# Going through eight weight columns in two runs of four instead of one run of eight

## The chip, the cores and the metric

The kernel runs on one core of a Trainium2 chip. The core has a matmul engine (TensorE, PE in the profile; its loads of stationary weights are PEld), three engines for elementwise work (VectorE or DVE, ScalarE or ACT, GpSimd or POOL) and SyncE (SP), which issues all DMAs here. Each engine works through its own instructions in order; semaphores order them between engines. The metric is the time of one execution on the device in microseconds, the median of several runs.

## The reference, cut to what matters

```python
def sm_attn(qq, kk, vv):                       # softmax(scale * qq kk^T) vv
    s = scale * np.matmul(qq, kk.transpose(0, 1, 3, 2))
    a = np.exp(s - np.max(s, axis=-1, keepdims=True))
    return np.matmul(a / (np.sum(a, axis=-1, keepdims=True) + 1e-09), vv)

p_packed = sm_attn(p, k, v)                    # 32 packed tokens per head
x = sm_attn(q, p_packed, p_packed)             # 8 batches, 8 heads, 576 tokens, 64 wide
x = x.transpose(0, 2, 1, 3).reshape(4608, 512)
h = x @ w_in                                   # 512 -> 2048
x = (np.maximum(h, 0) + alpha * np.minimum(h, 0)) @ w_out       # 2048 -> 512
g = x @ w_gate                                 # 512 -> 1536
return (g / (1 + np.exp(-g)) * (x @ w_val)) @ w_out2            # 1536 -> 512
```

The weights come as 64-bit floats. The kernel makes 32-bit floats of them on the chip and then splits each into a high and a low part, so that three fast matmuls (high by high, low by high, high by low) give a product of nearly full precision.

## The kernel before, in words

**Tiling.** The 4608 tokens are taken as 16 half batches `j` of 288 tokens, two for each of the 8 batches. The 2048 columns of the first layer are 16 blocks `f` of 128. A unit is one pair (`j`, `f`): `h_unit` (line 983) makes h for 128 columns and 288 tokens with 6 matmuls, ACT makes `m` (line 1003), DVE makes `g` (line 1006), ACT and POOL split g (lines 1014 and 1016), and three iterations later `o_unit` (line 1019) multiplies g by 128 rows of `w_out` with 12 matmuls into four PSUM banks `acc0` to `acc3`. The list `order` (line 872) says which units follow each other; there are 256.

**Projection.** The attention's second product is folded into the first layer: `pp_win(b, j)` (line 773) multiplies the packed tokens of batch b by four columns f of `w_in` and leaves a high and a low part (`ppw`). In the scripts `w02` means batch 0, columns 8 to 11, `w03` columns 12 to 15. There are four buffers of `ppw`.

**Runs.** The first two batches (four half batches) are computed while `w_in` and `w_out` are still being converted, so they don't go through all 16 columns at once. They go through columns 0 to 7 for each of the four half batches (units 0 to 31) and then through columns 8 to 15 (units 32 to 63). At the end of a run (`stop`) the four banks are evicted: at the end of a first run ACT and DVE copy them (lines 1051 and 1049) and SP stores them as partial sums `x1p` (line 1052); for the second run `load_part` (line 978) loads the partial sums back (line 981), DVE adds the banks to them (line 1047) and SP stores the result `x1d`. The tiles for this have the tag `x` with two buffers, which one half batch uses both. The first `o_unit` of a new run is put off by one iteration, so that the eviction has time. The later batches go through all 16 columns in one run.

**Conversion.** `convert()` (line 269) takes the next of 32 pieces (16 of `w_in`, 16 of `w_out`, in the order of `ORDER`), each 512 KB: a DMA (line 217), one or two ACT operations, five DVE operations (lines 224, 228, 237, 246, 254; pieces in `BY_POOL` have the last one on ACT and POOL), a POOL addition (line 265), and for `w_out` two ACT operations and a POOL operation more (lines 283 to 285). The work space is three raw buffers and five value buffers in `raw_tiles` and in one tile of tag `v`. `HOLD` puts the first ACT operation of some pieces behind the `m` of a given unit.

**Order of the work.** `EARLY` is a script by (iteration, 0 before or 1 after the `h_unit`): a `1` converts one piece, `w..` is a projection, the others are steps of the attention of batches 0 and 1. The attention of batch 2 is spread over units 36 to 62 by `STEPS`. A scheduler that simulates the engines sets the order of instructions within each engine from this program order, so a step can run some iterations away from its place. From iteration `CHAIN0` = 36 on every step is issued only behind the previous unit's `m` and `g` and the rounding of the one before (line 1288). From half-iteration `GROUP0` = 84 on (iteration 42) `more_weights2` (line 962) converts the second layer's weights in steps, up to two in each half-iteration, in the scratch of the first conversion, and stores them to DRAM (`wgvd`, `wo2d`); a tile of that scratch's tag is used again for the second layer's input at half-iteration 489.

Of the kernel before, what the change touches and what calls it, by code (L numbers as in the profile page):

```python
# [8 lines left out]
F32 = mybir.dt.float32  # L9
# [8 lines left out]
P = 128  # L18
# [27 lines left out]
    (13, 0): "d.a2",  # L46
    (15, 0): "c.a2",
    (17, 1): "w11",
    (18, 1): "1 1",
    (20, 1): "1 1",  # L50
    (21, 1): "1",
    (23, 1): "1",
    (24, 1): "1",
    (25, 1): "1 1",
    (26, 1): "1 1",
    (27, 1): "1 w02",
    (28, 1): "w03",
    (33, 1): "1",
    (36, 1): "w12 w13",
    (37, 1): "1 1",  # L60
}

ORDER = """
    i2 o2 i0 i3 i1 o0 o3 o1 i5 i4 i7 i6 o5 o4 o7 o6
    i13 i10 i11 o13 i15 i8 i14 i9 i12 o10 o14 o8 o9 o12 o11 o15
"""

BEHIND = {"c.k": 3, "c.q": 4, "c.v": 5, "d.k": 5, "d.q": 6, "d.v": 9}

BY_POOL = {0, 2, 4, 7, 11, 18, 23, 29}  # L70
HOLD = {15: 5, 16: 7, 17: 15, 19: 16}


STEPS = """
# [12 lines left out]

GROUP0 = 84  # L90


FIRST_X = dict(load=-36, A11=-27, S=-26, S2=-25, A12=-12, D4=-11, S3=-11, S1=-10, A22=-8, S4=-7)
# [11 lines left out]
def f32(ap):  # L105
    return ap.bitcast(F32)
# [3 lines left out]
def tile_kernel(  # L110
# [24 lines left out]
    B, H, S, D = q.shape  # L135
    NP = p.shape[2]
    NT, DM = out.shape
    KC = DM // P
    NF1 = alpha.shape[0] // P
# [6 lines left out]
    HS = S // 2  # L146
    NBLK = NT // (2 * T)
    NQ = H // HQ
    NHALF = 2 * B
# [3 lines left out]
    dram = ctx.enter_context(tc.tile_pool(name="dram", bufs=1, space=DRAM))  # L153
# [16 lines left out]
    def utile(tag, shape, name, dt=F32):  # L170
        return upool.tile(shape, dt, tag=tag, name=name, bufs=UBUFS[tag])
# [32 lines left out]
    def like(ap, other):  # L204

        return ap if len(other.shape) == 2 else ap.rearrange("p (c f) -> p c f", c=KC)
# [4 lines left out]
    def use(*cut):  # L211
        raws[:] = sum((r for r, _ in cut), [])
        vals[:] = sum((v for _, v in cut), [])

    def widen(src, raw, val, out=None, n_piece=-1):

        issued.append(nc.sync.dma_start(out=like(raw, src), in_=src))
        words = raw.rearrange("p (n t) -> p n t", t=2)
        low, high = words[:, :, 0], words[:, :, 1]
        held = n_piece in HOLD  # L220
        with tc.issue_after(begun[HOLD[n_piece]].ins) if held else ExitStack():
            nc.scalar.activation(out=f32(val), in_=f32(high), func=AF.Abs)
        yield "v"
        nc.vector.tensor_scalar(
            out=f32(val), in0=f32(val), scalar1=E_TOP, scalar2=E_LOW, op0=ALU.min, op1=ALU.max
        )
        yield "v"
        nc.vector.tensor_scalar(
            out=val,
            in0=val,  # L230
            scalar1=3,
            scalar2=0x3FFFFFF8,
            op0=ALU.logical_shift_left,
            op1=ALU.bitwise_and,
        )
        yield "v"
        nc.vector.scalar_tensor_tensor(
            out=val,
            in0=high,
            scalar=0xC0000000,  # L240
            in1=val,
            op0=ALU.bitwise_and,
            op1=ALU.bitwise_or,
        )
        yield "v"
        nc.vector.tensor_scalar(
            out=high, in0=val, scalar1=0xFF800000, scalar2=None, op0=ALU.bitwise_and
        )
        yield "v"
        if n_piece in BY_POOL:  # L250
            nc.scalar.activation(out=f32(low), in_=low, func=AF.Copy, scale=2.0**-52)
            nc.gpsimd.tensor_tensor(out=f32(low), in0=f32(low), in1=f32(high), op=ALU.mult)
        else:
            nc.vector.scalar_tensor_tensor(
                out=f32(low),
                in0=low,
                scalar=2.0**-52,
                in1=f32(high),
                op0=ALU.mult,
                op1=ALU.mult,  # L260
            )
        yield "p"
        full = f32(val) if out is None else like(f32(val), out)
        other = f32(low) if out is None else like(f32(low), out)
        nc.gpsimd.tensor_tensor(  # L265
            out=full if out is None else out, in0=full, in1=other, op=ALU.add
        )

    def convert(n=1):

        for src, parts, f in queue[:n]:
            raw, val = raws.pop(0), vals.pop(0)
            raws.append(raw)
            vals.append(val)
            n_piece = len(issued)
            dst = parts()
            light = len(dst) == 1
            for _ in widen(src, raw, val, dst[0] if light else None, n_piece):
                pass
            if not light:  # L280
                hi, lo = dst
                full = like(f32(val), hi)
                nc.scalar.activation(out=full, in_=full, func=AF.Copy, scale=sg[:, f : f + 1])
                nc.scalar.activation(out=hi, in_=full, func=AF.Copy)
                nc.gpsimd.tensor_tensor(out=lo, in0=full, in1=f32(hi), op=ALU.subtract)
        del queue[:n]
# [7 lines left out]
    def cut_up(t, raws):  # L294

        n = t.shape[1]
        return (
            [t[:, 1024 * i : 1024 * (i + 1)] for i in range(raws)],
            [t[:, c : c + 512] for c in range(1024 * raws, n, 512)],
        )  # L300
# [248 lines left out]
    def behind():  # L549

        return tc.issue_after(before[-1].ins) if before else ExitStack()

    def done(last):
        if chained:
            before[:] = [last]
# [250 lines left out]
    for f in range(NF1):  # L806
# [4 lines left out]
    space = cut_up(raw_tiles[0], 2), cut_up(raw_tiles[1], 1)  # L811
# [4 lines left out]
        b=quad(1, ["h"], evac=nc.vector),  # L816
# [11 lines left out]
    def run(script):  # L828
        for word in script.split():
            if word == "1":  # L830
                convert()
            elif word[0] == "w":
                pp_win(int(word[1]), int(word[2]))
            else:
                n, step = word.split(".")
                if step == "pd":
                    groups[n][step](pd[:, dense[n][0], :], dense[n][1])
                else:
                    groups[n][step]()
# [26 lines left out]
    def at(it, late, fn):  # L866

        plan.setdefault((it, late), []).append(fn)

    order = []
    for bs in [(0, 1)] + [(b,) for b in range(2, B)]:
        for fs in (range(NF1 // 2), range(NF1 // 2, NF1)) if len(bs) > 1 else (range(NF1),):
            for j in range(2 * bs[0], 2 * bs[-1] + 2):
                order += [(j, f, f == fs[0], f == fs[-1]) for f in fs]

    NB1 = 2 * NF1
    busy = set()
# [96 lines left out]
    x1p = {}  # L976

    def load_part(j):
        part[j] = [utile("x", [P, 2, HS], f"x1p{j}_{pr}") for pr in range(2)]
        for pr in range(2):  # L980
            nc.sync.dma_start(out=part[j][pr], in_=x1p[j][:, 2 * pr : 2 * pr + 2, :])
# [37 lines left out]
    def o_unit(it):  # L1019
        j, f, start, stop = order[it]  # L1020
        ghi, glo = gs.pop(it)
        hi, lo = wout[f // WP]
        for dc in range(KC):
            if start:
                acc[dc] = ps.tile([P, 512], F32, tag=f"acc{dc}", name=f"acc{dc}_{it}")[:, :HS]
        with behind():
            for dc in range(KC):
                c = slice(dc * P, (dc + 1) * P)
                nc.tensor.matmul(acc[dc], lo[:, f % WP, c], ghi, start=start, stop=False)  # L1029
                last = nc.tensor.matmul(acc[dc], hi[:, f % WP, c], ghi, start=False, stop=False)  # L1030
        done(last)
        with behind():
            for dc in range(KC):
                c = slice(dc * P, (dc + 1) * P)
                last = nc.tensor.matmul(acc[dc], hi[:, f % WP, c], glo, start=False, stop=stop)  # L1035
        done(last)
        if not stop:
            return
        if f != NF1 - 1:
            x1p[j] = dram.tile([P, KC, HS], F32, name=f"x1p{j}")  # L1040
        dst = x1d[j] if f == NF1 - 1 else x1p[j]
        for pr in range(2):
            xs = part[j][pr] if j in part else utile("x", [P, 2, HS], f"x1s{it}_{pr}")
            for i in range(2):
                a = acc[2 * pr + i]
                if j in part:
                    nc.vector.tensor_tensor(out=xs[:, i, :], in0=a, in1=xs[:, i, :], op=ALU.add)
                elif i:
                    nc.vector.tensor_copy(out=xs[:, i, :], in_=a)
                else:  # L1050
                    nc.scalar.activation(out=xs[:, i, :], in_=a, func=AF.Copy)
            nc.sync.dma_start(out=dst[:, 2 * pr : 2 * pr + 2, :], in_=xs)

    for j in range(4):
        at(NB1 + 8 * j + 6, 0, lambda j=j: load_part(j))


    raw2, xs2, gvw, wo2, ps2, acc2, outs = {}, {}, {}, {}, {}, {}, {}
# [229 lines left out]
    def steps(it, late):  # L1288


        with ExitStack() as held:
# [6 lines left out]
            slot = 2 * it + late  # L1298
            if slot >= GROUP0:
                more_weights2(slot not in busy)  # L1300
# [59 lines left out]
```

## Time and profile before

| | us |
|---|---|
| median of 3 runs | 1701.05 |
| lowest and highest | 1701.03 and 1706.88 |
| the profiled execution, whole | 1702.91 |
| its span in the trace | 1701.1 |
| PE busy | 1609.9 (95%) |
| DVE busy | 868.2 (51%) |
| ACT busy | 683.0 (40%) |
| POOL busy | 708.8 (42%) |

The span runs from the first to the last instruction. Busy time of an engine doesn't say what bounds a stage; for this the idle time of the engine that does the most, and what ended it, is read by stretch. In this document stretches are cut at 139.85, 192.63, 246.41 and 281 us, where the activation of line 1003 of units 18, 34, 51 and 63 starts. The granted clock (PEclk) is the share of full speed that the matmul engine got.

### The profile page before, as it was taken

How to read it: one execution, taken by the hardware profiler on the slowest of the kernel's cores; microseconds unless marked ns; L12 is line 12 of the kernel's file. 1: busy time of each engine (PE TensorE's matmuls, PEld its weight loads, DVE VectorE, ACT ScalarE, POOL GpSimd, SP SyncE). 2: the span in 40 equal slices, each digit the busy share in tenths (PEclk: the TensorE clock that was granted, in tenths of full speed). 3: DMA queues.
4: the chain of work that ended last, by engine and by line, in shares of the span. 5: the costliest groups of instructions: out<-in, count | busy, mean ns of one | idle time of the engine just before them, and what ended most of it. 6: DMA issues, size and time to landing. Idle time of an engine off the chain costs nothing.

```text
span 1701.1 us, 28474 instructions
## 1 busy us (share of the span) xinstructions
PE 1609.9 (95%) x10708; PEld 1456.6 (86%) x10708; DVE 868.2 (51%) x1549; ACT 683.0 (40%) x1511; POOL 708.8 (42%) x752
## 2 busy tenths in 40 slices
PE   5688899999999989999899999999999999999997
PEld 3467798988888888889899999999999999999997
DVE  6999757565756656565533443443443343244222
ACT  5774645555544555454522232232232232123122
POOL 3556744565554654547622322322322222232222
PEclk7799999999999999999999999999999999999999
DMA  9433464635445362644573463465455456445442
GB/s 238 121 102 115 120 159 115 165 95 155 130 108 143 117 156 53 150 138 139 182 274 141 177 237 139 166 202 185 164 211 182 158 191 202 159 174 185 156 173 81
DMA packets 227369, 266.11 MB, mean 156 GB/s; under 512 B 130464, under 2 KB 189856, under 8 KB 227232
## 3 DMA queue, kind: packets, MB, share of 16 engines
q1 hardware_dynamic: 227232, 264.30, 49.2%
q8 instruction: 84, 1.38, 0.3%
q14 instruction: 53, 0.43, 0.1%
HBM read 214.70 MB, written 49.55 MB: 155 GB/s over the span
## 4 chain that ended last, share of the span: by engine, by line
issue 39%; PE 25%; POOL 17%; DMA 7%; DVE 6%; ACT 4%; SPq 1%; POOLq 0%; ACTq 0%; DVEq 0%
POOL pl L1247 8%; PE acc L1029 5%; PE acc L1030 5%; PE acc L1035 5%; POOL s L1227 4%; DMA wgvd<-cva 4%; PE h L305 3%; PE h L307 2%; PE h L306 2%; POOL lo L1016 1%; DMA cva<-in_moe_w_gate_dram 1%; POOL cva L934 1%; DVE g L1006 1%; PE ppw L564 1%; POOL cva L265 1%
## 5 line engine op out<-in xcount | busy, mean ns | idle before, releaser
L1016 POOL TENSOR_TENSOR lo<-g,hi 128x288 fp32r<-128x288 f32 x256 | 227.5, 890 | 240.6 <-ACT hi L1014 187.8
L1227 POOL TENSOR_TENSOR s<-s,u 128x384 f32<-128x384 f32 x72 | 73.0, 1014 | 489.9 <-ACT s L1221 489.9
L1006 DVE SCALAR_TENSOR_TENSOR g<-h,sg,m 128x288 f32<-128x288 f32 x256 | 130.3, 509 | 162.2 <-ACT m L1003 132.0
L1184 DVE TENSOR_TENSOR u<-yb,p 128x384 f32<-128x384 f32 x144 | 80.1, 556 | 255.6 <-PE yb L307 255.6
L1247 POOL TENSOR_TENSOR pl<-s,ph 128x384 fp32r<-128x384 f32 x144 | 145.5, 1032 | 106.4 <-ACT ph L1245 106.4
L305 PE MATMUL h<-a2h,ppw 128*128 128x288 f32 x512 | 163.2, 319 | 27.0 <-DVE g L1006 21.4
L1184 DVE TENSOR_TENSOR u<-vb,u 128x384 f32<-128x384 f32 x144 | 80.4, 558 | 197.3 <-PE vb L307 196.9
L1014 ACT ACTIVATE hi<-g 128x288 fp32r<-128x288 f32 x256 | 113.1, 442 | 155.5 <-DVE g L1006 149.1
L307 PE MATMUL o<-wp,ph 128*128 128x512 f32 x432 | 171.5, 397 | 0.0
L306 PE MATMUL o<-wp,ph 128*128 128x512 f32 x432 | 170.9, 396 | 0.0
L305 PE MATMUL o<-wp,pl 128*128 128x512 f32 x432 | 168.8, 391 | 0.9 <-POOL pl L1247 0.9
L1221 ACT ACTIVATE s<-p 128x384 f32<-128x384 f32 x72 | 37.9, 526 | 302.0 <-DVE p L1184 302.0
L307 PE MATMUL h<-a2l,ppw 128*128 128x288 f32 x512 | 153.0, 299 | 0.0
L306 PE MATMUL h<-a2h,ppw 128*128 128x288 f32 x512 | 152.5, 298 | 0.0
L305 PEld LDWEIGHTS h<-a2h,ppw 128*128 128x128 f32 x512 | 97.9, 191 | 62.4 <-DVE g L1006 33.0
L305 PE MATMUL yb<-ring,gv 128*128 128x384 f32 x432 | 146.0, 338 | 0.2
L307 PE MATMUL yb<-ring,gv 128*128 128x384 f32 x432 | 144.4, 334 | 0.0
L306 PE MATMUL yb<-ring,gv 128*128 128x384 f32 x432 | 144.4, 334 | 0.0
L1003 ACT ACTIVATE m<-h,sal 128x288 f32<-128x288 f32 x256 | 125.6, 492 | 41.5 <-PE h L307 40.6
L1245 ACT ACTIVATE ph<-s 128x384 fp32r<-128x384 f32 x144 | 69.8, 519 | 121.3 <-DVE s L1225 121.3
L307 PEld LDWEIGHTS h<-a2l,ppw 128*128 128x128 f32 x512 | 98.0, 191 | 0.8 <-issue 0.8
L306 PEld LDWEIGHTS h<-a2h,ppw 128*128 128x128 f32 x512 | 98.4, 192 | 0.0
(232 smaller groups left out, 4187.1 us busy)
## 6 DMA issues: line engine op xcount, KB each, us to landing
gv<-wgvd SPq DMA_DIRECT2D x144, 896.0 KB, 6.2
wgvd<-cva SPq DMA_DIRECT2D x84, 256.0 KB, 2.6
cva<-in_moe_w_out_dram SPq DMA_DIRECT2D x28, 512.0 KB, 3.8
v<-in_v_dram SPq DMA_DIRECT2D x16, 576.0 KB, 5.4
out_dram<-os SPq DMA_DIRECT2D x12, 768.0 KB, 3.8
cva<-in_moe_w_in_dram SPq DMA_DIRECT2D x16, 512.0 KB, 3.9
kr<-in_k_dram SPq DMA_DIRECT2D x96, 72.0 KB, 2.8
qr<-in_q_dram SPq DMA_DIRECT2D x96, 72.0 KB, 2.5
```

Of the source, the lines that this page charges most:

```text
L305: nc.tensor.matmul(o, wlo, xhi, start=start, stop=False, **kw)
L306: nc.tensor.matmul(o, whi, xhi, start=False, stop=False, **kw)
L307: return nc.tensor.matmul(o, whi, xlo, start=False, stop=stop, **kw)
L1003: begun[it] = nc.scalar.activation(out=m, in_=hp, func=AF.Copy, scale=sal[:, f : f + 1])
L1006: made[it] = nc.vector.scalar_tensor_tensor(out=g32, in0=hp, scalar=sg[:, f : f + 1], in1=m, op0=ALU.mult, op1=ALU.max)
L1014: rounded[n] = nc.scalar.activation(out=hi, in_=x, func=AF.Copy)
L1016: nc.gpsimd.tensor_tensor(out=lo, in0=x, in1=f32(hi), op=ALU.subtract)
L1029: nc.tensor.matmul(acc[dc], lo[:, f % WP, c], ghi, start=start, stop=False)
L1030: last = nc.tensor.matmul(acc[dc], hi[:, f % WP, c], ghi, start=False, stop=False)
L1184: return nc.vector.tensor_tensor(out=out, in0=bank, in1=x, op=ALU.add)
L1227: latest.append(nc.gpsimd.tensor_tensor(out=s2, in0=s2, in1=u3, op=ALU.mult))
L1247: nc.gpsimd.tensor_tensor(out=lo, in0=x, in1=f32(hi), op=ALU.subtract)
```

## The change

The list of units of the first two batches is given by a table `RUNS`: columns 0 to 7 of the four half batches, then 8 to 11 of the four, then 12 to 15 of the four. Each half batch now ends three runs instead of two; the end after column 11 adds to the partial sums and stores them again under a new DRAM name. A `load_part` is placed at the iteration of the last unit of each run after the first (units 35, 39, 43, 47 and 51, 55, 59, 63) instead of at iterations 38, 46, 54 and 62. The conversions from iteration 18 on are spread differently, the projections `w02`, `w03`, `w12` and `w13` move, a word `D` takes the tile of tag `v` out of the work space at iteration 37, columns 8 to 11 are converted before 12 to 15, one `HOLD` is two units later, and `GROUP0` is 90 instead of 84 (iteration 45).

```diff
     (17, 1): "w11",
-    (18, 1): "1 1",
-    (20, 1): "1 1",
+    (18, 1): "1",
+    (20, 1): "1",
     (21, 1): "1",
     (23, 1): "1",
     (24, 1): "1",
-    (25, 1): "1 1",
-    (26, 1): "1 1",
-    (27, 1): "1 w02",
-    (28, 1): "w03",
-    (33, 1): "1",
-    (36, 1): "w12 w13",
-    (37, 1): "1 1",
+    (25, 1): "1",
+    (26, 1): "w02",
+    (27, 1): "1",
+    (29, 1): "1",
+    (31, 1): "1",
+    (33, 1): "1 w12",
+    (34, 1): "1",
+    (35, 1): "1",
+    (36, 1): "1",
+    (37, 0): "D",
+    (39, 1): "1",
+    (41, 1): "1 w03",
+    (43, 1): "1",
+    (50, 1): "w13",
 }
 ORDER = """
     i2 o2 i0 i3 i1 o0 o3 o1 i5 i4 i7 i6 o5 o4 o7 o6
-    i13 i10 i11 o13 i15 i8 i14 i9 i12 o10 o14 o8 o9 o12 o11 o15
+    i8 i9 i10 i11 o8 o9 o10 o11 i12 i13 i14 i15 o12 o13 o14 o15
 """
-HOLD = {15: 5, 16: 7, 17: 15, 19: 16}
+HOLD = {15: 5, 16: 7, 17: 15, 19: 18}
+
+RUNS = ((0, 1, 2, 3), 0, 8), ((0, 1, 2, 3), 8, 12), ((0, 1, 2, 3), 12, 16)
-GROUP0 = 84
+GROUP0 = 90
+            elif word == "D":
+                use(*space)
-    order = []
-    for bs in [(0, 1)] + [(b,) for b in range(2, B)]:
-        for fs in (range(NF1 // 2), range(NF1 // 2, NF1)) if len(bs) > 1 else (range(NF1),):
-            for j in range(2 * bs[0], 2 * bs[-1] + 2):
-                order += [(j, f, f == fs[0], f == fs[-1]) for f in fs]
+    order, again = [], []
+    for js, f0, f1 in RUNS + tuple(((j,), 0, NF1) for j in range(4, NHALF)):
+        for j in js:
+            if f0:
+                again.append((len(order) + f1 - f0 - 1, j))
+            order += [(j, f, f == f0, f == f1 - 1) for f in range(f0, f1)]
         if f != NF1 - 1:
-            x1p[j] = dram.tile([P, KC, HS], F32, name=f"x1p{j}")
+            x1p[j] = dram.tile([P, KC, HS], F32, name=f"x1p{j}_{f}")
-    for j in range(4):
-        at(NB1 + 8 * j + 6, 0, lambda j=j: load_part(j))
+    for it, j in again:
+        at(it, 0, lambda j=j: load_part(j))
```

## Rows read from the trace of the kernel before

**Rows 1.** The page: the span, and each engine's busy time.
```profile
span 1701.1 us, 28474 instructions
...
PE 1609.9 (95%) x10708; PEld 1456.6 (86%) x10708; DVE 868.2 (51%) x1549; ACT 683.0 (40%) x1511; POOL 708.8 (42%) x752
```

**Rows 2.** Stretches: us, busy us (xinstructions) by engine, granted clock, DMA share, GB/s.
```profile
139.85:192.63 52.78, 45.63 (x305) 39.52 (x304) 47.31 (x70) 29.40 (x62) 37.22 (x32) 0.97 0.39 122
192.63:246.41 53.78, 49.15 (x461) 43.45 (x467) 31.09 (x65) 29.46 (x70) 27.37 (x31) 1.00 0.59 141
246.41:281.00 34.59, 34.34 (x298) 29.93 (x284) 25.39 (x46) 18.64 (x41) 19.93 (x23) 1.00 0.51 146
sum 141.15, PE 129.12 PEld 112.91 DVE 103.78 ACT 77.50 POOL 84.52; mean PE 43.04 PEld 37.64 DVE 34.59 ACT 25.83 POOL 28.17
```

**Rows 3.** Waits of PE, 139.85 to 281: waiter, releaser, us, times, longest.
```profile
PE h L305 <- DVE g L1006: 5.1, 6, 2.2
PE ppw L795 <- DVE ppw L800: 3.5, 2, 3.0
PE acc L1029 <- DVE x1s L1049: 3.0, 1, 3.0
```

**Rows 4.** Timeline of PE: start, us, instruction [idle before, releaser].
```profile
161.83 0.40 PE L305 MATMUL h<-a2h,ppw 128*128 128x288 f32 x1 [2.16 <-DVE g L1006]
...
167.42 0.37 PE L1029 MATMUL acc<-hi,wo0l 128*128 128x288 f32 x1 [3.04 <-DVE x1s L1049]
...
200.04 1.08 PE L795 MATMUL ppw<-wi,ppT 128*64 128x512 f32 x4 [3.05 <-DVE ppw L800]
```

**Rows 5.** Stretches of 1 us after 168, and 200 to 204.
```profile
168.00:169.00 1.00, 1.00 (x5) 0.38 (x5) 1.00 (x4) 0.23 (x1) 0.00 (x0) 0.54 0.84 317
...
171.00:172.00 1.00, 1.00 (x6) 0.25 (x3) 0.93 (x3) 1.00 (x3) 1.00 (x1) 0.76 0.00 0
...
200.00:204.00 4.00, 3.50 (x18) 1.81 (x19) 4.00 (x9) 1.24 (x3) 0.00 (x0) 1.00 0.89 222
```

**Rows 6.** DVE by line, 139.85 to 192.63: busy us, mean ns, idle before.
```profile
L254 DVE SCALAR_TENSOR_TENSOR cva<-cva 128x512 f32<-128x512 uint32 x8 | 7.5, 938 | 0.0
...
L237 DVE SCALAR_TENSOR_TENSOR cva<-cva,cva 128x512 uint32<-128x512 uint32 x1 | 1.2, 1164 | 0.0
```

**Rows 7.** DVE by line, 192.63 to 246.41.
```profile
L254 DVE SCALAR_TENSOR_TENSOR cva<-cva 128x512 f32<-128x512 uint32 x4 | 3.1, 801 | 0.0
...
L237 DVE SCALAR_TENSOR_TENSOR cva<-cva 128x512 uint32<-128x512 uint32 x2 | 1.4, 682 | 0.0
```

**Rows 8.** Additions of partial sums: the group (ns), and three run ends in the timeline.
```profile
L1047 DVE TENSOR_TENSOR x1p<-acc,x1p x16: 420/448/457, 223.3 to 295.6; 128x288 f32<-128x288 f32 x16
...
223.33 1.54 DVE L1047 TENSOR_TENSOR x1p<-acc,x1p 128x288 f32<-128x288 f32 x4
...
245.16 1.55 DVE L1047 TENSOR_TENSOR x1p<-acc,x1p 128x288 f32<-128x288 f32 x4
...
269.92 1.51 DVE L1047 TENSOR_TENSOR x1p<-acc,x1p 128x288 f32<-128x288 f32 x4
```

**Rows 9.** Timeline of SP: issues of stores and loads of partial sums.
```profile
224.17 1.07 SPq L1052 DMA_DIRECT2D x1d<-x1p  x2
226.31 1.09 SPq L981 DMA_DIRECT2D x1p<-x1p  x2
...
249.79 1.69 SPq L981 DMA_DIRECT2D x1p<-x1p  x2
...
275.35 0.33 SPq L981 DMA_DIRECT2D x1p<-x1p  x1
```

**Rows 10.** The tile x1p, 212 to 300: from issue to landing.
```profile
DMA to landing us min/median/max: 2.1/2.7/3.9
```

**Rows 11.** Waits of SP's queue, 212.62 to 281.
```profile
SPq L1052 <- DVE x1p L1047: 17.9, 4, 8.6
```

**Rows 12.** Last store of the second layer's weights (SP), first product after (PE).
```profile
845.61 1.66 SPq L947 DMA_DIRECT2D wo2d<-cva  x2
...
859.46 0.34 PE L305 MATMUL xb<-ring,gv 128*128 128x384 f32 x1
```

## The prediction

> **What bounds the kernel now.** The page comes first: the span is 1701.1 us and the matmul engine (PE) is busy 95% of it [rows 1]. So a change can only win where PE stands idle, or runs at half clock. The diff touches the first 64 units (a unit is one `h_unit` and, three iterations later, one `o_unit`), so the next view is the busy time by stretch, cut at the starts of units 18, 34, 51 and 63 [rows 2]. In the first stretch PE is busy 45.63 of 52.78 us while VectorE (DVE) is busy 47.31: idle 7.15 us. In the second it is idle 53.78 - 49.15 = 4.63, in the third 0.25. Together 12.0 us of 141.15; this is nearly all that the change can win. The waits of PE say what ends the idle time [rows 3]: 5.1 us for `g` from DVE (line 1006), 3.5 us for the residual of a projected weight from DVE (line 800), 3.0 us for the eviction of a run's sums by DVE (line 1049). All three are DVE. The timeline shows the three largest gaps: 2.16 us before a unit at 161.83, 3.04 us at a run's end at 167.42, 3.05 us between the two projections of unit 36 at 200.04 [rows 4]. [...]
>
> What fills DVE: ten rows of the first stretch belong to weight conversion (lines 224 to 254; 7.5 us down to 1.2 us, 39.0 us in all, about 9 pieces, 4.3 us a piece) ([rows 6], first and last of the ten). In the second stretch six such rows sum to 11.0 us for 4 pieces, 2.75 us a piece ([rows 7], first and last of the six).
>
> **The change, part by part.**
>
> *Conversions moved (first stretch).* Before, the script starts 11 pieces from iteration 18 to 26, then 2 by 33, then 2 at 37. After, it is 6 by iteration 25 and 9 more from 27 to 41; the tenth, at 43, finds the queue empty. Since pieces run up to a few iterations behind their slot, I take 3 pieces out of the first stretch. [...] Idle 7.15 plus clock 1.7 is 8.9 us. It can't fall below nothing, and it can stay as it is if `g` still queues behind a conversion in DVE's order. I keep 2 us (a 0.8 us wait at some units, and part of one eviction's wait), because the third stretch, with DVE at 25.39 of 34.59 us (73%), idles 0.25 us [rows 2]. Term: -7.0, bounds -8.9 and 0.
>
> *Projections split.* `w12 w13` ran back to back at iteration 36 with two PSUM buffers, so the second waited for the evictions of the first: 3.05 us at 200.04, and 0.46 us more within the 3.5 us of line 800 [rows 3, 4]. Now `w02`, `w12`, `w03` and `w13` stand at 26, 33, 41 and 50, each alone. Their matmuls stay the same in number. Term: -3.0, bounds -3.5 and 0 (a lone one can still wait for DVE).
>
> *Conversions moved (second stretch).* The same 3 pieces come to iterations 34 to 51: +8.3 us by 2.75, +12.9 us by 4.3. They lie beside PE work, but DVE was at 31.09 of 53.78 us; with these and with 8 of the new additions (8 x 0.448 = 3.6 us [rows 8]) it comes to 43 to 47.6 us, against 49.15 us of PE work. That is 87 to 97%, as full as the first stretch was before (47.31 of 52.78, 90%, with 7.15 us idle). What speaks for less: from iteration 36 on each step is issued only behind the previous unit's `m`, `g` and rounding (`CHAIN0`), so `g` goes ahead of conversions. Bounds 0 and +8 us; I take +3.5, nearer to the third stretch's 0.25 than to 7.15.
>
> The first row of conversion says why the price of a piece differs: line 254 takes 938 ns in the first stretch and 801 ns in the second [rows 6, 7], with GpSimd (POOL) busy 37.22 of 52.78 us and 27.37 of 53.78 us [rows 2]. [...]
>
> *Four more run ends.* Each of the four half batches now ends a run after column 11 too: 4 x 4 additions x 0.448 us = 7.1 us of DVE [rows 8], 8 stores and 8 loads of 288 KB. PE gets no matmul more; it waits only if an eviction is late, since the first `o_unit` of a new run is put off by one iteration, which leaves two `h_unit`s to cover the four additions of 1.5 us. The risk is the turnaround: the `x` tiles have two buffers, both used by one half batch, so the next partial sums can be loaded only after the last ones are stored. In the trace the stores follow the first addition within 1 us and the loads are issued at 226.31, 249.79 and 275.35 [rows 9]; with a landing of 2.7 us (at most 3.9) [rows 10] the last load has landed 6.5 to 9.9 us after the first addition (223.33, 245.16, 269.92 [rows 8]). Run ends were 8 units apart, 21.8 and 24.8 us; they will be 4 apart, 10.9 to 12.4 us. So 1.0 to 5.9 us are to spare. Bounds 0 and +17 (below, second rival); I take +1.0 for the odd late one.
>
> *SP's queue.* SP issues in order; stores waited 17.9 us in 4 waits for their additions, up to 8.6 us [rows 11], and twice as many will stand there. Behind them are raw weights, K, Q and V of batch 2 and the stores of the second layer's weights. None of these shows among PE's waits [rows 3], so the cover is there; if it goes, it shows as DVE waiting for K or Q. Taken at 0 (within the bounds of the last term).
>
> *Second layer's weights three iterations later (`GROUP0`).* The scripts' last step moves by 5 half-iterations. Its last stores are issued at 845.61, the first product of the next stage starts at 859.46 [rows 12]: 13.8 us apart, while 2.5 iterations at 10.9 to 12.4 us for four are 7 to 8 us. Taken at 0, bounds -2 and +5 (all later conflicts shift in phase too).
>
> *`HOLD`, `ORDER`, the `D` word, new DRAM names:* the order only follows the runs, and `D` gives the shared scratch back before V of batch 2 is loaded. Cost 0; the cover is that columns 12 to 15 are needed only at iteration 48.
>
> Sum: -7.0 - 3.0 + 3.5 + 1.0 = -5.5 us. The profiled execution took 1702.91 us for a span of 1701.1 us (1.8 us lie around it), the median is 1701.05. So the span should be 1695.6, and the median of runs 1701.05 - 5.5 = 1695.6 us.
>
> **The rivals.**
>
> *All of the idle time goes.* The second stretch takes the added DVE work as the third took its own, with about 0 idle, and the run ends cost nothing: -7.0 - 3.0 - 1.0 (half of the 2 us kept) = -11 us, 1690 us. For it: the chained order. Against: DVE near 90% has come with idle PE elsewhere.
>
> *The stall only moves.* Total DVE work rises by 7.1 us and no piece is removed; the second stretch then idles as the first did, +8, and run ends cost 2: net 0, 1701 us. For it: 87 to 97%. Against: the chain order and the split projections, which don't depend on DVE's share.
>
> *Turnaround too long (the other side).* Place: the 7 loads of partial sums that follow another run's additions, 4 units before. If SP holds the store or load so that the turn is 13.5 us instead of 6.5 to 9.9, each end comes 2.5 us late after the spare time is used, the additions block DVE's queue and PE waits for the banks: 7 x 2.5 = 17.5, 1713 us. It decides from 0.8 us per end (5.5 / 7). For it: one hold of 8.6 us at a store. Against: holds end when the additions are done, and loads went out 2 to 5 us after them. Rows show what a late end adds beyond its idle time: after 3.04 us idle the clock fell, after 3.05 us at 200.04 it stayed at 1.00 [rows 4, 5]. [...]
>
> **How the numbers follow.** Forecast 0.45 (1691 to 1700), all idle time gone 0.25 (1690), stall only moves 0.17 (1701), turnaround 0.13 (1713). A measurement tells 0.5%, 8.5 us, from no change: faster is below 1692.5, slower above 1709.6. Faster: 0.25 and 0.07 of the forecast's low end, 0.32. Slower: 0.13. Same: 0.55. The range for 8 in 10 takes the idle time gone with the clock's 1.7 and a favourable phase (-15, 1686) and half of the turnaround's price (1707).
>
> **What would show it.** In the changed trace: PE idle from unit 18 to 34 about 2 us; no gap of 3 us between projections; idle from 34 to 51 about 5 us with DVE at 43 us or more; 32 rather than 16 additions of line 1047's kind, none waiting on a load of `x1p`. The prediction is wrong if the wait for a load ends PE's idle time at several run ends, if the first stretch still idles 6 us, or if idle time grows after unit 66.

## The result and the profile after

The changed kernel takes 1712.05 us (median of 9 runs, 1707.58 to 1719.71). The kernel before, run beside it, takes 1704.74 us (9 runs). The ratio is 1.0055, 95% interval 1.0037 to 1.0072: about 9 us slower. The forecast was 5.5 us faster, and 1712 lies above the range's upper end of 1707. The sign was wrong.

The page of the changed kernel, span and busy time by engine (its profiled execution took 1714.91 us):

```profile
span 1712.9 us, 28519 instructions
...
PE 1622.1 (95%) x10708; PEld 1465.1 (86%) x10708; DVE 873.1 (51%) x1565; ACT 683.4 (40%) x1511; POOL 704.5 (41%) x752
```

PE has the same 10708 matmuls as in [rows 1] and is busy 12.2 us longer, so it must run slower somewhere. The stretches, cut at units 18, 34, 51 and 63 of this kernel, and below them three windows of 2 us; the columns are those of [rows 2]:

```profile
138.66:192.45 53.79, 48.12 (x302) 41.10 (x301) 45.72 (x67) 26.67 (x57) 36.39 (x33) 0.94 0.38 120
192.45:256.47 64.02, 55.72 (x466) 48.57 (x472) 38.58 (x75) 30.23 (x69) 25.16 (x26) 0.89 0.58 151
256.47:290.93 34.46, 34.46 (x301) 30.27 (x294) 27.92 (x53) 19.01 (x42) 20.16 (x24) 1.00 0.62 184
...
218.00:220.00 2.00, 2.00 (x9) 2.00 (x9) 1.01 (x3) 1.06 (x3) 1.01 (x1) 0.50 0.00 0
...
248.00:250.00 2.00, 0.00 (x0) 0.00 (x0) 1.09 (x3) 1.64 (x4) 0.00 (x0) 0.92 0.15 42
...
252.00:254.00 2.00, 2.00 (x10) 2.00 (x9) 0.11 (x1) 0.28 (x1) 0.00 (x0) 0.50 0.00 0
```

The second stretch takes 64.02 us instead of 53.78; the first is 1.0 us longer and the third 0.1 us shorter. The best single measure of a stretch is what PE loses in it: its length less busy time times granted clock, so that idle time and half clock count alike. Before, this was 52.78 - 45.63 x 0.97 = 8.5, then 4.6 and 0.3 us, 13.4 in all. After, it is 53.79 - 48.12 x 0.94 = 8.6, then 64.02 - 55.72 x 0.89 = 14.4, then 0: 23.0 in all. These 9.6 us are about the measured slowdown, and all of them lie between units 34 and 51. The spans of the two profiled executions differ by 11.8 us: the changed kernel's is 1.2 us shorter before unit 18, 11.1 longer from unit 18 to 63, 2.8 shorter from there to unit 252, and 4.7 longer from unit 252 to the end. The last figure comes back under `GROUP0` below.

What PE waited for from unit 18 to 63 (columns as in [rows 3]):

```profile
PE h L314 <- DVE g L1018: 5.6, 5, 1.9
PE ppt L635 <- DVE ppw L809: 4.8, 1, 4.8
PE s L573 <- DVE ppw L809: 2.1, 1, 2.1
PE s L573 <- DVE kT L623: 1.4, 1, 1.4
```

The wait of one projection for another is gone, and so is the one for a run's eviction (3.5 and 3.0 us in [rows 3]). In their place the attention of batch 2 (`s`, `ppt`) waits for the eviction of a projection (`ppw`), 2.1 and 4.8 us. The timeline of the engines around both places shows why:

```profile
211.07 1.67 DVE L246 SCALAR_TENSOR_TENSOR cva<-cva,cva 128x512 uint32<-128x512 uint32 x1
212.78 0.91 DVE L255 TENSOR_SCALAR cva<-cva 128x512 uint32<-128x512 uint32 x1
213.72 0.69 DVE L263 SCALAR_TENSOR_TENSOR cva<-cva 128x512 f32<-128x512 uint32 x1
...
214.76 0.68 DVE L809 TENSOR_TENSOR ppw<-ppw,ppw 128x512 fp32r<-128x512 f32 x1
...
215.49 2.27 PE L573 MATMUL s<-kT,pT 64*32 64x288 f32 x16 [2.05 <-DVE ppw L809]
...
242.05 0.38 SPq L226 DMA_DIRECT2D cva<-in_moe_w_val_dram  x1
...
244.82 1.94 PE L804 MATMUL ppw<-wi,ppT 128*64 128x512 f32 x8
...
248.20 0.66 ACT L231 ACTIVATE cva<-cva 128x512 f32<-128x512 f32 x1 [5.01 <-DMA cva<-in_moe_w_val_dram]
...
249.15 0.59 ACT L808 ACTIVATE ppw<-ppw 128x512 fp32r<-128x512 f32 x1
...
251.57 0.48 PE L635 MATMUL ppt<-ident,ppbd 128*128 128x128 f32 x1 [4.81 <-DVE ppw L809]
```

`pp_win` writes two PSUM tiles of tag `at`, of which there are two, and the attention steps use the same tag. From `CHAIN0` (iteration 36) on, PE's order is fixed by the script. `w03` at (41, 1) stands directly ahead of the second score matrix `s1b`, and `w13` at (50, 1) directly ahead of `ppt`; each of these needs a bank that is not evicted yet. At `w03` the eviction on DVE (line 809) came behind conversion operations (211.07 to 214.4) and one `g`. At `w13` it was worse: the eviction on ACT (line 808) stood behind the first operation of a second-layer weight (line 231), which waited at the head of ACT's queue 5.01 us for a load issued at 242.05. The wait was passed on: line 808 had its data when the matmuls ended near 246.8 and started at 249.15, behind line 231. After each gap the granted clock is low: 0.50 in the windows from 218 and from 252, against 1.00 over all of the second stretch before.

The four further run ends are there, and no PE wait has a load of `x1p` or an addition to it as its releaser. One of them still costs something: the wait of 1.4 us for K (`s <- kT`) ends with a transposition of K on DVE that stands behind the four additions of the first new run end and one conversion operation.

```profile
203.61 1.54 DVE L1059 TENSOR_TENSOR x1p<-acc,x1p 128x288 f32<-128x288 f32 x4
205.07 0.91 DVE L237 TENSOR_SCALAR cva<-cva 128x512 uint32<-128x512 uint32 x1
205.90 0.77 DVE L623 STREAM_TRANSPOSE kT<-kr 128x576 f32<-128x576 f32 x1
...
206.72 0.68 PE L573 MATMUL s<-kT,pT 64*32 64x288 f32 x4 [1.44 <-DVE kT L623]
```

The group of additions over the whole span, as in [rows 8] but 32 instead of 16:

```profile
L1059 DVE TENSOR_TENSOR x1p<-acc,x1p x32: 418/447/459, 203.6 to 302.8; 128x288 f32<-128x288 f32 x32
```

### The profile page after: what moved, and what is told of

The parts are those of the page before. It is cut to its first block, busy times and chain, and to the rows that moved or that the text cites. A ratio compares the mean times of both kernels' runs of the same rounds, so it can differ in the third digit from the quotient of the medians.

```text
span 1712.9 us, 28519 instructions
## 1 busy us (share of the span) xinstructions
PE 1622.1 (95%) x10708; PEld 1465.1 (86%) x10708; DVE 873.1 (51%) x1565; ACT 683.4 (40%) x1511; POOL 704.5 (41%) x752
## 4 chain that ended last, share of the span: by engine, by line
issue 40%; PE 22%; POOL 18%; DMA 8%; DVE 5%; ACT 3%; SPq 2%; POOLq 0%; ACTq 0%; DVEq 0%
POOL pl L1259 8%; PE acc L1041 4%; PE acc L1047 4%; PE acc L1042 4%; DMA wgvd<-cva 4%; POOL s L1239 4%; PE h L314 2%; PE h L316 2%; PE h L315 2%; POOL lo L1028 2%; DMA cva<-in_moe_w_val_dram 2%; POOL cva L274 1%; POOL cva L946 1%; PE ppw L573 1%; DMA cva<-in_moe_w_gate_dram 1%
```

## The experiments

Theory A: the 10 us come from where `w03` and `w13` stand, ahead of attention steps that need the same banks. Rival B: they come from the run ends (additions, stores, loads) or from conversion work in the second stretch. A table first, then each run. "Lost" is the measure above in the profiled execution; medians of before in these comparisons were 1703.13 to 1705.61 us. Up to unit 34 the changed kernel, e2, e4 and e7 have the same script, and they lost 8.6, 7.0, 7.5 and 8.7 us there: so much do single executions differ.

| kernel | ratio to before, interval | lost 18-34 | 34-51 | 51-63 | sum |
|---|---|---|---|---|---|
| before | 1 | 8.5 | 4.6 | 0.3 | 13.4 |
| after | 1.0055 (1.0037 to 1.0072) | 8.6 | 14.4 | 0.0 | 23.0 |
| e1_proj_early | 1.0023 (1.0010 to 1.0036) | 9.0 | 4.2 | 0.8 | 14.0 |
| e2_proj_gap | 0.9992 (0.9978 to 1.0005) | 7.0 | 2.2 | 0.5 | 9.7 |
| e3_runs_only | 1.0020 (1.0006 to 1.0035) | 8.4 | 6.1 | 0.9 | 15.5 |
| e4_group84 | 1.0023 (1.0011 to 1.0036) | 7.5 | 7.5 | 0.1 | 15.1 |
| e7_gap_group84 | 0.9997 (0.9986 to 1.0007) | 8.7 | 1.8 | 2.4 | 12.9 |
| e6_before_split | 1.0028 (1.0015 to 1.0040) | 8.7 | 9.9 | 0.0 | 18.6 |
| e5_later_pieces | 1.0002 (0.9991 to 1.0014) | 5.0 | 6.0 | 3.1 | 14.1 |
| e8_later_gap | 1.0044 (1.0032 to 1.0057) | 4.7 | 14.2 | 2.9 | 21.8 |
| e9_later_w03 | 1.0006 (0.9993 to 1.0018) | 4.7 | 6.2 | 1.8 | 12.7 |
| e10_pause | 0.9985 (0.9975 to 0.9996) | 5.8 | 2.4 | 0.0 | 8.2 |
| e12_group87 | 0.9975 (0.9962 to 0.9988) | 5.7 | 2.8 | 0.7 | 9.2 |

**e2_proj_gap: the two projections in places free of attention.** From the changed kernel:

```diff
+    (38, 1): "w03",
-    (41, 1): "1 w03",
+    (41, 1): "1",
-    (50, 1): "w13",
+    (47, 0): "w13",
```

> The changed kernel, with w03 at iteration 38 (between the attention's pt at 37 and s1a at 40) and w13 at 47 (between et1 at 45 and pp1 at 49); both still in the part with a fixed order, but no attention step that takes the two PSUM banks follows at once. Theory A: the two gaps go or shrink under 1 us, units 34 to 51 take 54 to 58 us, 0.996 to 1.002 of before. If a fixed order alone is enough, whatever follows: gaps of 2 to 5 us move to the places of the projections, 1.003 to 1.006. Theory B: as the changed kernel, 1.004 to 1.007.

Measured: 0.9992. The second stretch (34 to 51) of this kernel, and PE's waits from unit 34 to 63:

```profile
192.90:245.42 52.52, 50.29 (x466) 43.68 (x466) 36.41 (x72) 29.96 (x69) 24.50 (x26) 1.00 0.70 181
```

```profile
PE et L688 <- ACT E L668: 1.1, 1, 1.1
PE h L315 <- DVE g L1019: 1.0, 3, 0.4
PE s L574 <- ACT E L656: 0.5, 1, 0.5
```

Two moved words take the stretch from 64.02 to 52.52 us, with the run ends and the conversions as they were. The wait for K is gone as well; the matmuls of `w03`, 1.94 us, now stand ahead of the score matrix. Theory A holds; B as the main cause falls.

**e1_proj_early: both projections before the attention starts**, `w03` at (35, 1) and `w13` at (36, 1).

```diff
+    (35, 1): "1 w03",
+    (36, 1): "1 w13",
-    (41, 1): "1 w03",
+    (41, 1): "1",
-    (50, 1): "w13",
```

> The changed kernel, with projection w03 at iteration 35 (instead of 41) and w13 at 36 (instead of 50); nothing else moved. Theory A (projections: from iteration 36 on the matmul engine's order is fixed, w03 and w13 stand directly ahead of attention steps that need the same two PSUM banks, their evictions stand in ACT's and DVE's queues behind conversions and a weight load, PE stops 2.05 and 4.81 us and the clock halves after each): units 34 to 51 take 53 to 57 us instead of 64.0, no gap of 2 us or more before the attention's matmuls, the time is 0.995 to 1.001 of the kernel before. Theory B (four more run ends hold SP's queue, 22.1 us in 3 waits, and delay weight, K, Q and V loads): units 34 to 51 stay at 62 to 65 us, 1.004 to 1.007 of before.

Measured: 1.0023, between the two expectations. Both gaps are gone, but the lost time is 14.0 us in all instead of e2's 9.7, and `s` waits once, 2.7 us, for ACT (and 0.9 us for K). Why this place is worse than e2's was not followed further.

```profile
PE s L572 <- ACT ppT_2b L721: 2.7, 1, 2.7
PE s L572 <- DVE kT L622: 0.9, 1, 0.9
```

**e4_group84: the changed kernel with `GROUP0 = 84`**, which shifts the second-layer load away from `w13`.

```diff
-GROUP0 = 90
+GROUP0 = 84
```

> The changed kernel, with the second layer's weights started at half-iteration 84 again instead of 90. Theory A, with the weight load as the reason of the longer gap (ACT waited 5.0 us for w_val at the head of its queue, the eviction of w13 behind it): the gap of 4.81 us at w13 changes to under 2 us or moves, the gap of 2.05 us at w03 stays, 1.001 to 1.005 of before. If the second layer's start doesn't matter: both gaps stay, 1.004 to 1.007.

Measured: 1.0023. The timeline shows that the wait at `w03` stays and the one at `w13` shrinks from 4.81 to 0.76 us:

```profile
216.78 0.69 PE L573 MATMUL s<-kT,pT 64*32 64x288 f32 x8 [2.05 <-DVE ppw L809]
...
249.01 0.33 PE L635 MATMUL ppt<-ident,ppbd 128*128 128x128 f32 x1 [0.76 <-DVE ppw L809]
```

So the load at the head of ACT's queue is what made `w13` dear: 1.0055 to 1.0023.

**e7_gap_group84: e2 with `GROUP0 = 84`** (from e2).

```diff
-GROUP0 = 90
+GROUP0 = 84
```

> The run with projections in the gaps, with the second layer's weights started at half-iteration 84 instead of 90. If the start matters only through what stands behind its weight loads in ACT's queue: no difference from the run at 90 within 0.2%, 0.997 to 1.001 of before. If a later start costs by itself (phase against the attention of later batches, the tail before the second layer): 2 us or more faster, 0.995 to 0.998.

Measured: 0.9997 against e2's 0.9992: by itself the start of the second layer's weights is worth nothing that can be told. From e4 to e7 only the two projections move, and the kernel gets 0.26% faster.

**e3_runs_only: the kernel before with the run table alone** (`RUNS`, `again`, the DRAM names; script, order and `GROUP0` as before).

```diff
+RUNS = ((0, 1, 2, 3), 0, 8), ((0, 1, 2, 3), 8, 12), ((0, 1, 2, 3), 12, 16)
-    order = []
...
+    order, again = [], []
...
-            x1p[j] = dram.tile([P, KC, HS], F32, name=f"x1p{j}")
+            x1p[j] = dram.tile([P, KC, HS], F32, name=f"x1p{j}_{f}")
...
```

> The kernel before with the two runs of four alone: order of units, loads and stores of partial sums as in the changed kernel; script of conversions and projections, order of pieces and start of the second layer's weights as before. Theory A: the four more run ends cost next to nothing, units 34 to 51 take 52 to 56 us (53.8 before), 0.999 to 1.002 of before. Theory B: most of the loss is there, 1.004 or more, and PE waits for additions or for loads of partial sums, 1 us or more at several run ends.

Measured: 1.0020, about 3 us. A late end is seen, but no load of partial sums is late:

```profile
237.06 0.66 ACT L224 ACTIVATE cva<-cva 128x512 f32<-128x512 f32 x1 [2.83 <-DMA cva<-in_moe_w_val_dram]
...
237.76 0.43 DVE L226 TENSOR_SCALAR cva<-cva 128x512 f32<-128x512 f32 x1 [2.43 <-ACT cva L224]
238.10 1.18 DVE L1050 TENSOR_TENSOR x1p<-acc,x1p 128x288 f32<-128x288 f32 x3
...
238.61 0.40 PE L1032 MATMUL acc<-hi,wo2l 128*128 128x288 f32 x1 [1.52 <-DVE x1p L1050]
```

Again a weight load holds ACT, ACT holds DVE, and the additions that free PE's banks stand behind it. PE's waits for such additions are 2.3 us in all, and the lost time is 2.1 us more than before.

**e6_before_split: the kernel before with its pair `w12 w13` at 36 taken apart.**

```diff
-    (36, 1): "w12 w13",
+    (38, 1): "w12",
+    (47, 0): "w13",
```

> The kernel before with w12 at iteration 38 and w13 at 47 instead of both at 36; nothing else. The prediction's term for the split alone (-3.0 us): units 34 to 42 take about 5 us less (3.5 us of idle time and part of w13's matmuls move out), units 42 to 51 at most 2.5 us more, 0.997 to 0.999 of before. Rival (a projection in the fixed order always costs its evictions' wait): 0.999 to 1.002.

Measured: 1.0028. The gap of 3.05 us [rows 4] is gone, but PE then waits for the last pieces of `w_out`:

```profile
210.94 0.61 PE L1030 MATMUL acc<-hi,wo2l 128*128 128x288 f32 x1 [6.29 <-POOL wo2l L286]
```

In the kernel before the same wait is 0.56 us at 209.87. The gap covered a deadline: all of columns 8 to 15 had to be ready by unit 39. The run table needs columns 12 to 15 later, which would let the split pay; no run tests these two together without the other moves.

**e5_later_pieces: fewer conversions before unit 34.** From e2:

```diff
-    (21, 1): "1",
-    (23, 1): "1",
+    (22, 1): "1",
     (24, 1): "1",
-    (25, 1): "1",
-    (26, 1): "w02",
-    (27, 1): "1",
-    (29, 1): "1",
-    (31, 1): "1",
-    (33, 1): "1 w12",
+    (26, 1): "1 w02",
+    (28, 1): "1",
+    (30, 1): "1",
+    (32, 1): "1",
+    (33, 1): "w12",
     (34, 1): "1",
-    (35, 1): "1",
     (36, 1): "1",
     (37, 0): "D",
-    (38, 1): "w03",
+    (38, 1): "1",
     (39, 1): "1",
     (41, 1): "1",
-    (43, 1): "1",
-    (47, 0): "w13",
+    (42, 1): "1",
+    (44, 1): "1",
+    (46, 1): "w03",
+    (47, 1): "w13",
```

> As the run with projections in the gaps, but with pieces started two iterations apart from 18 to 32 (18, 20, 22, 24, 26, 28, 30, 32) and the last seven at 34, 36, 38, 39, 41, 42 and 44; w02 at 26, w12 at 33, w03 at 46, w13 at 47. So some three pieces fewer are started before iteration 34. Theory A1 (VectorE's share bounds units 18 to 34, and the changed kernel gained nothing there since it converted as many pieces in them as the kernel before): fewer pieces are converted in that stretch (7 or less against 9) and it takes 49 to 52 us instead of 53.3, with the later stretches at most 2 us longer; 0.996 to 0.999 of before. Rival (g waits behind single conversion operations in VectorE's queue, however few there are): the stretch stays at 52.5 to 54 us and the time at 0.998 to 1.002.

Measured: 1.0002. The three stretches:

```profile
140.88:189.01 48.13, 44.97 (x293) 38.88 (x292) 34.50 (x52) 24.02 (x54) 30.28 (x29) 0.96 0.39 114
189.01:247.40 58.39, 55.75 (x491) 48.91 (x490) 47.07 (x87) 32.76 (x73) 31.40 (x30) 0.94 0.72 188
247.40:283.67 36.27, 33.17 (x276) 28.79 (x275) 28.29 (x55) 18.64 (x44) 20.41 (x24) 1.00 0.57 165
```

The first stretch of e2, to compare:

```profile
139.60:192.90 53.30, 46.28 (x308) 39.77 (x307) 45.98 (x68) 26.50 (x57) 36.08 (x32) 1.00 0.40 121
```

DVE falls from 45.98 (e2) to 34.50 us in the first stretch, and PE loses 5.0 instead of 7.0 us there. But then it loses 9.1 instead of 2.7 us, among this a wait of 2.4 us of the first score matrix for K (`PE s <- DVE kT`). The last transposition of K stands behind the four additions of a run end (1.62 us) and one conversion operation (0.41 us). What the first stretch gave is paid back.

**e8_later_gap: e5 with the projections elsewhere.**

```diff
+    (39, 0): "w03",
-    (46, 1): "w03",
-    (47, 1): "w13",
+    (47, 0): "w13",
```

> The later pieces of e5_later_pieces together with projections in steps that don't meet the attention: w02 at 26, w12 at 33, w03 at (39, 0), w13 at (47, 0). Theory A (the places of w03 and w13 cost the 10 us, and the pieces of the first stretch cost 5 us there): units 18 to 34 take about 48 us as in e5, units 34 to 51 about 53 us as in e2, no PE wait for ppw over 1 us; ratio to before 0.995 to 0.998. Rival (what is taken out of the first stretch is always paid back: DVE has the same work in all): units 34 to 63 take 3 us or more longer than in e2 (87.3 us), ratio 0.999 or more.

Measured: 1.0044, a miss of my own making: with the later pieces, `w03` comes before its columns are converted.

```profile
206.47 3.68 PE L804 MATMUL ppw<-wi,ppT 128*64 128x512 f32 x8 [7.78 <-POOL wi L274]
```

**e9_later_w03: e8 with `w03` later.**

```diff
-    (39, 0): "w03",
-    (44, 1): "1",
+    (44, 1): "1 w03",
```

> e8_later_gap with w03 at (44, 1) instead of (39, 0). In e8 PE waited 7.8 us at 206.47 for the fourth of the columns 12 to 15 of w_in (PE ppw <- POOL wi), a wait that my placing of w03 made. Theory A: that wait goes, units 18 to 34 stay at 48 us, the kT wait of e5 (2.4 us) stays, units 34 to 51 take 55 to 57 us; ratio 0.998 to 1.000. Rival (DVE's added work in units 34 to 63 takes back whatever the first stretch gives): units 34 to 63 take 5 us more than in e2 (87.3), ratio 0.999 to 1.002.

Measured: 1.0006, as the rival had it: that wait is gone, the one for K is still there, and units 34 to 63 take 94.2 us against e2's 87.4 (units 18 to 63 in all 142.5 against 140.7). The profiled execution, 1700.80 us, is the shortest of 12, and their median is 1707.36 us, so this trace is not of a typical one.

```profile
PE s L572 <- DVE kT L622: 2.4, 1, 2.4
```

**e10_pause: e9 without a piece between iterations 36 and 40, where K is prepared.**

```diff
-    (33, 1): "w12",
+    (33, 1): "1 w12",
     (34, 1): "1",
+    (35, 1): "1",
     (36, 1): "1",
     (37, 0): "D",
-    (38, 1): "1",
-    (39, 1): "1",
-    (41, 1): "1",
+    (40, 1): "1",
     (42, 1): "1",
```

> e9_later_w03 with no piece between iterations 36 and 40, where the first score matrix of batch 2 waited for K in e5 (PE s <- DVE kT, 2.4 us): pieces at 33, 34, 35 and 36, then 40, 42 and 44. Theory A: units 18 to 34 about 49 us, no kT wait, units 34 to 51 53 to 55 us; ratio 0.995 to 0.998. Rival (paid back): units 18 to 63 in all as in e2 (140.6 us) within 1.5 us; ratio 0.998 to 1.001.

Measured: 0.9985, a little faster than before; it is within the rival's range, and the interval touches A's. Neither holds in full: units 18 to 63 take 138.3 us, 2.4 less than in e2, but the wait for K is 1.2 us instead of none. No conversion operation stands ahead of K any more, only the additions of the run end:

```profile
201.24 1.51 DVE L1057 TENSOR_TENSOR x1p<-acc,x1p 128x288 f32<-128x288 f32 x4
202.88 0.78 DVE L621 STREAM_TRANSPOSE kT<-kr 128x576 f32<-128x576 f32 x1
```

The sum of lost time, 8.2 us, is the lowest of all.

**e12_group87: e10 with the second layer's weights half way.**

```diff
-GROUP0 = 90
+GROUP0 = 87
```

> e10_pause with GROUP0 = 87, half way. Theory A (only the end counts): the wait for gv goes or halves, ratio to before 0.997 to 0.9985. Rival (what is saved at the end is paid in units 42 to 63): ratio 0.998 to 0.9995. If neither end matters and only the phase does: within 0.1 per cent of e10's 0.9985.

Measured: 1701.25 us, ratio 0.9975 (0.9962 to 0.9988), the fastest of all: 0.25% below before, 0.8% below the changed kernel (0.9975 / 1.0055). It isn't told apart from e10, and all three expectations allow this ratio, so it doesn't decide between them; PE's wait for `gv` is 0.9 instead of 1.2 us. Its three stretches:

```profile
138.38:189.54 51.16, 46.89 (x300) 39.75 (x299) 42.41 (x62) 24.88 (x54) 33.63 (x30) 0.97 0.37 116
189.54:242.96 53.42, 50.65 (x468) 44.54 (x474) 42.54 (x82) 31.64 (x73) 30.52 (x31) 1.00 0.74 195
242.96:278.16 35.20, 34.48 (x298) 30.03 (x286) 26.61 (x52) 18.62 (x42) 16.62 (x22) 1.00 0.59 174
```

DVE is busy 42.54 us in the second stretch, 4 us more than in the changed kernel, and yet PE loses 2.8 instead of 14.4 us: what stands ahead of whom decides there, not DVE's share.

A further run, e11_group84 (e10 with `GROUP0 = 84`), starts the second layer's weights while the last two pieces (iterations 42 and 44) still use the same scratch. It computes something else than the reference, most likely for this reason, and nothing is drawn from its time.

## Why the prediction was wrong, step by step

**"Projections split. Term: -3.0, bounds -3.5 and 0." The step that failed.** The removal was right: the 3.05 us gap and the 3.5 us of waits are gone. But the new places were taken as free, and the bounds excluded a loss. Shown: `w03` and `w13`, each alone, cost 2.05 and 4.81 us of idle time and the clock after each: the second stretch loses 14.4 us against e2's 2.2. Moving only these two words gives 1.0055 to 0.9992 (e2), 0.63% or 10.7 us. The prediction did name the two PSUM buffers as the reason of the old gap; it did not go on to ask who else uses them from iteration 36 on. The attention steps of `STEPS` do, and the kernel's text shows both lists. Of the 15 us between the forecast and the measured time, by the lost time, about 9 lie in the second stretch, where this step failed, and about 7 in the first, which is the next step.

**"Conversions moved (first stretch). I take 3 pieces out. Term: -7.0."** Wrong by 7 us: the lost time is 8.6 us, as before. DVE is busy 45.72 us there, 1.6 us less than before and not the 12.9 us less of three pieces of 4.3 us: counted by the POOL addition that ends a piece, nine such additions start between units 18 and 34 in both kernels, though the script has 13 pieces at iterations 18 to 33 before and 10 after. A script's place limits when a piece may start, and pieces ran behind their places before. That the term exists is shown by e5, where six start there: 5.0 us lost. That it is a gain of the whole is not shown: e5, e8 and e9 pay it back, and e10 and e12 keep some in their lost time, but their ratios are not told apart from that of e2. The 1.7 us of clock in this term, and in the range, is what the trace of the kernel before shows after its gap at 167.42: 0.46 and 0.24 us by the first and last of four windows [rows 5] and 0.50 in each of the two between, which follow here. That this would be won too was the author's estimate; in the changed kernel the stretch loses 48.12 x (1 - 0.94) = 2.9 us to the clock.

```profile
169.00:170.00 1.00, 1.00 (x4) 0.24 (x2) 1.00 (x3) 0.21 (x1) 0.71 (x1) 0.50 0.87 332
170.00:171.00 1.00, 1.00 (x6) 0.24 (x2) 1.00 (x2) 0.63 (x2) 0.37 (x2) 0.50 0.06 23
```

**"Conversions moved (second stretch). +3.5, bounds 0 and +8."** The stretch loses 9.8 us more, but not by DVE's share: DVE is busy 38.58 of 64.02 us, and e2 and e12 lose 2 to 3 us with 36.41 of 52.52 and 42.54 of 53.42 us. The term's condition did not occur, as no pieces came over from the first stretch. Where they did, in e5 and e9 (DVE busy 47.07 of 58.39 and 49.81 of 59.10 us), the stretch lost 6.0 and 6.2 us, 3.8 and 4.0 more than in e2 and near the term; but 2.4 us of it is the wait for K.

**"Four more run ends. +1.0."** Alone (e3) they cost about 3 us, within the bounds but by another way than the turnaround: the additions queued behind a wait for a weight load. In the changed kernel the third stretch, with two run ends more than before, takes 34.46 us against 34.59: nothing. The first new run end, ahead of K, is the one that shows: 1.4 us there, 1.2 us in e10. The term had about the right size.

**The rival "Turnaround too long"** gave 1713, nearly the measured number, by a mechanism that did not occur: no PE wait of the changed kernel ends with a load of partial sums or with an addition to them. That the number fits is luck. That a gap can also cost clock, as its rows have it, did hold: the clock was 0.50 from 218 to 220 and from 252 to 254, after 2.05 and 4.81 us idle.

**"SP's queue, 0" and "`GROUP0`, 0."** SP's stores waited longer for additions (22.1 us in 3 waits from unit 34 to 51, against 17.9 in 4 in [rows 11]), and no PE wait follows from it that I could trace. `GROUP0` is 0 by itself as far as the medians tell (e7 against e2), but it set when the load came that held ACT at `w13`; there it was worth 0.3% (e4). And it is not free at the change of stage. There PE waits about 1 us for a weight that it had in time before, and the last stores of weights come 9.4 us before the first product instead of 13.8 [rows 12]:

```profile
PE xb L314 <- DMA gv<-wgvd: 1.0, 1, 1.0
...
859.49 1.67 SPq L959 DMA_DIRECT2D wo2d<-cva  x2
...
868.88 0.34 PE L314 MATMUL xb<-ring,gv 128*128 128x384 f32 x1
```

From the start of unit 252 to the end, the kernels with `GROUP0 = 84` take 851.9 to 854.3 us (before 852.9), those with 90 take 855.1 to 857.6 (the changed kernel 857.6), and e12 with 87 takes 854.8. In the two pairs that differ in `GROUP0` alone the later start costs 2.3 us there (e2 against e7) and 5.7 us (the changed kernel against e4); e2 saves 3.2 us against e7 between units 18 and 63. These are single executions.

What stays open: e10 and e12 differ from before by 0.15 and 0.25%, of which the lost time between units 18 and 63 (5.2 and 4.2 us less) would explain all and more. Part of it is given back after unit 252, where they take 3.8 and 1.9 us more than before; the rest isn't followed. All lost times are of one execution each, and executions of one kernel differ by some us.

## What to carry to other kernels

A step that uses a shared PSUM tag must be placed against every other user of the tag, not only against its old neighbour: list the users in program order and ask which engine evicts the bank and what stands at the head of that engine's queue. An elementwise operation that waits for a DMA belongs behind the evictions that PE needs, for its wait becomes theirs: behind line 231, which waited 5.01 us, the eviction of line 808 started 2.4 us after the matmuls it needed had ended. And before removing a visible gap, ask which deadline it covers (e6).

## What the runs showed of the hardware

A gap can cost more than its length, and its length alone does not tell how much. After 4.81 us idle the clock was 0.50 in the window of 252 to 254, after only 2.05 us it was 0.50 from 218 to 220, while after 3.05 us at 200.04 in the kernel before it stayed at 1.00 [rows 4, 5]. In all, the second stretch lost 64.02 - 55.72 = 8.3 us to idle time and 6.1 us to the clock.

A 512 KB load of `w_val` took 6.1 us from issue to landing in the changed kernel (issued at 242.05), 6.9 us in e3 (230.11) and 5.0 us in the kernel before (229.7). What sets the difference is not shown.

In the kernel before, line 254 took 0.65 to 0.69 us in each of the nine single records from 60 to 247 us that have no POOL instruction beside them. Of the eleven that have one, three took 0.68 to 0.69 us and eight 0.88 to 1.49 us.
